# A linear-attention and bilinear feed-forward kernel: the same steps and loads in another written-out order

## The chip, the core and the metric

The kernel runs on one core of a Trainium2 chip. The core has a matrix engine (TensorE, PE in the profile; its weight loads are shown apart as PEld), a vector engine (VectorE, DVE), a scalar engine (ScalarE, ACT), a general engine (GpSimd, POOL) and a queue engine that only issues transfers (SyncE, SP). Each has its own list of instructions and works through it in the order written; semaphores make one wait for another. Sixteen DMA engines move data between the chip's memory and the on-chip buffer. Matmul results go to PSUM, eight banks of 512 float32 columns by 128 rows. The metric is the device time in microseconds (us) of one execution.

## The reference

Two parts follow each other: a gated linear attention, step by step over the sequence, and a feed-forward block without an activation function, in which two products are multiplied element by element.

```python
B, H, S, D = 4, 8, 768, 48          # q, k, v, alpha: [B, H, S, D]
for t in range(S):
    state = alpha[:, :, t, :, None] * state + einsum('bhd,bhe->bhde', k[:, :, t], v[:, :, t])
    y[:, :, t] = einsum('bhd,bhde->bhe', q[:, :, t], state)
x = y.transpose(0, 2, 1, 3).reshape(B * S, H * D)     # [3072, 384]
out = ((x @ w_a) * (x @ w_b)) @ w_out                 # w_a, w_b: [384, 1536], w_out: [1536, 384]
```

## The kernel before

**Staging.** The sequence of 768 steps is cut into three stretches of 256, and the four batches into two pairs. That gives six chunks: chunk c holds stretch c // 2 for the batch pair c % 2 (line 503). Inside a chunk `u` is the batch of the pair (0 or 1), and `g` the half of the stretch. Steps are held in pairs (`r`), so that 128 rows hold 256 steps. Within a chunk the recurrence becomes matmuls: decays are summed in logarithms, queries and keys are scaled by their exponentials, scores between steps are masked and multiplied with the values, and a state carries what came earlier from one half or stretch to the next. The chunk's output is written transposed (`xT`, 384 features by 512 steps), and the feed-forward part runs on it: 12 slices `f` of 128 hidden columns.

**The order.** Nothing is planned when the program is built. The string `PROGRAM` (line 17) lists all operations in the order in which they are issued, with the number of the chunk ahead of the colon; lines 1033 to 1038 walk through it and call one small function per operation. The last letter of many operations names the engine: V vector, S scalar, P GpSimd, Y SyncE. A number at the end of a matmul operation is its PSUM bank; an operation that takes two banks names the first. Since each engine keeps the order of the list, the list settles what stands behind what on every engine and on the transfer queues of POOL and SP. An outside planner wrote the list with its own costs and rules; it is not part of the kernel.

The operations that the next sections name are these (function and line behind them):

- `ld`, `W`, `Wo`: loads of alpha, k, q, v (510), of columns of w_a and w_b (493), of rows of w_out (497). `cz`, `cs`, `cm`: constants. `fill n`: n dummy matmuls (538).
- `ln`, `ra`: logarithm and inverse of alpha on ACT (518, 606). `l2`, `l2s`: sums of two steps' logarithms (524, 575). `H`, `L`, `R`: the sums split into parts that the matmul takes without loss (560, 569, 584). `B`, `A2`, `AQ`: running sums by matmul (551, 601, 591). `E`: their exponentials on ACT (620).
- `lv`: k or q scaled by alpha or its inverse (613). `mk`, `mq`: k and q scaled by the exponentials (635). `dk`, `de`, or `dr`, `dl`: the decay over a half, by matmul and ACT (658, 684) or by two transfers (646, 653).
- `C`, `Ce`: a turn (transpose) by TensorE and its copy out of PSUM (696, 706). `T`, `Tr`: the turn by a transfer on SP and a copy (712, 715).
- `v`, `vs`: values cast and swapped between halves (732, 741).
- `K`, `K2`: the state's matmuls (750, 762), `k`: the state's update on vector (778).
- `D`: scores (798). `M`: scores masked by vector out of PSUM (812); or `Mc`, a copy by ACT (816), and `Mm`, the mask by vector (820).
- `SA`, `SB`: the part of the output from the state, `Y`: the part from the scores (837, 852). `X`: the copy to `xT` (864), for one half (`u`) of its columns.
- `a f w`, `b f w`: slice f of x @ w_a and x @ w_b, three matmuls each (885). w is `*` for all 512 columns of `xT`, or 0 or 1 for 256 of them. `as`: the copy of `a` by ACT (891). `pr`: the product of that copy with `b` by vector, into `prod` (897).
- `o m h`: half of the 12 matmuls of output rows m (905), `ot`: their copy out (930), `st`: the store (943). `oc`, `otc`, `stc`: the same for half the columns of the last rows.

Buffers are few. A PSUM bank is taken again as soon as the operation that empties it is done, so `pr`, `as`, `k`, `M`, `Ce`, `X`, `ot` and `E` let later matmuls go. `as` has three buffers (line 894), `ot` four (931), `prod` and `xT` two, the loaded tiles two for each tensor (403).

The lines that carry most of PE's time are one loop each:

```python
for kk in range(KT):          # 3; line 889
    nc.tensor.matmul(p, lhsT=(wa_t, wb_t)[w][:, kk, f * 128:(f + 1) * 128], rhs=ch.xT[:, kk, us, :], start=(kk == 0), stop=(kk == KT - 1))
for f in range(half * NFF // 2, (half + 1) * NFF // 2):     # 6; line 911
    nc.tensor.matmul(op, lhsT=ch.prod[:, f, at:at + C], rhs=wo_t[:, f, :], start=(f == 0), stop=(f == NFF - 1))
```

Of the kernel before, what the change touches and what calls it, by code (L numbers as in the profile page):

```python
# [17 lines left out]
0: cm 0; c1; cz 0 b P; ci; ld a 0b Y; c1a; ld a 0a Y; ln 0b; cu; cz 1 b P; fill 7 0; cu2 V; cz 0 q V; cus; ld k 0b Y; ld k 0a Y; B 0b 2; ln 0a  # L18
# [4 lines left out]
0: v 0 S; vs 0 1 S; B 1a 6; E 1a i; M 0 0  # L23
1: ld a 1 P
0: E 1a b; W a 768 1536; c2 P; vs 0 0 V; B 1b 4; W b 768 1536; dk 1 6; E 1b i; M 0 1
1: ld q 0 P
0: Y 0
1: ld k 0 P
0: mk 1a V; SA 0; E 1b b; mq 1a V; mk 1b V; C 1 0 7; K 1 1 2; mq 1b V; Ce 1 0 V; C 1 1 3; v 1 S; Ce 1 1 V; de 1; K 1 0 4; k 1 0 V; k 1 1 V; D 1 0 6; X 0 S
0: a 2 0 0; a 4 0 1; Mc 1 0; vs 1 1 V; as 4 0; vs 1 0 V; a 5 0 3; D 1 1 4; Mc 1 1; SB 1 6; Mm 1 1 V; a 1 0 1; Mm 1 0 V; b 4 0 2; as 1 0; pr 4 0; a 3 0 4; as 3 0  # L30
0: b 0 0 1; K 0 1 5; SA 1; Y 1; a 0 0 2; as 2 0; b 2 0 0; k 0 1 V; X 1 S; b 3 0 4; pr 3 0
1: ln 0; l2 0 P
0: b 1 0 5; pr 1 0; a 4 1 6; pr 2 0
1: ln 1
0: b 5 0 7
1: ld v 0 P; H 0 V
0: as 0 0; pr 0 0; as 5 0; pr 5 0
1: l2 1 P
0: a 2 1 4
1: ld q 1 P  # L40
0: Wo 0 6; a 1 1 5; a 0 1 0; as 0 1
1: ra 0; lv 0 q P
0: b 0 1 2; pr 0 1; a 10 * 3; a 7 * 0; as 4 1; b 4 1 1
1: L 0 V
0: pr 4 1; b 2 1 2; as 7 *
1: ld k 1 P
0: as 2 1; as 10 *
1: ra 1
0: pr 2 1
1: H 1 V  # L50
0: b 1 1 6; b 5 1 7; b 7 * 4
1: L 1 V
0: pr 7 *
1: A2 0 0; E 0 i; E 0 b; mq 0 V
0: b 10 * 1; pr 10 *
1: lv 0 k P
0: Wo 6 12; as 1 1; pr 1 1; a 8 * 2; a 5 1 3; as 5 1; pr 5 1; b 3 1 0; b 9 * 4; a 6 * 3
1: A2 1 5; E 1 b; E 1 i
0: a 9 * 1
2: ld a * P  # L60
1: mk 0 V
0: a 3 1 6; as 3 1; pr 3 1; a 11 * 7
1: dk * 5
0: as 8 *; as 9 *; pr 9 *
1: ld v 1 P; C 0 1 2; lv 1 q P
2: ld q * P
0: as 6 *
1: lv 1 k P; Ce 0 1 S; C 0 0 6; Ce 0 0 V
2: ld k * P
1: de *  # L70
0: b 8 * 0; pr 8 *
3: ld v * P
0: cz 1 v P
1: v 0 S
0: as 11 *; c3 P
1: vs 0 1 S
0: b 11 * 1; pr 11 *; b 6 * 2; pr 6 *
1: K2 0 0 0 3; k 0 0 V; D 0 0 4; Mc 0 0; Mm 0 0 V
0: o 2 0 6
1: mq 1 V  # L80
0: o 3 0 7
1: SB 0 0; vs 0 0 S
3: ld a * P
1: mk 1 V; D 0 1 4; M 0 1
0: o 1 0 2; o 1 1 -; ot 1 S
1: k 0 1 V
0: o 3 1 -
1: C 1 1 2; C 1 0 4
0: ot 3 V
1: Ce 1 1 V  # L90
0: st 3 Y
2: ln *; l2s 0 P
0: o 2 1 -
1: K2 1 1 5 7; Ce 1 0 V; D 1 1 2; Y 0; v 1 S; SA 0
0: o 0 0 4; o 0 1 -
1: vs 1 0 S
2: l2 0 V
1: Mc 1 1
2: l2s 1 V; R 0
1: X 0 S; a 4 0 0; vs 1 1 S; k 1 0 V  # L100
0: cs 1 0 P; ot 0 S; st 0 Y
2: R 1; ra 1
1: a 2 0 1
2: lv 1 q P
1: as 4 0; k 1 1 V; as 2 0; D 1 0 2; M 1 0
2: AQ 4; E 0 i
1: b 4 0 7; a 6 0 0
2: E 1 b
1: b 6 0 1; a 1 0 2; pr 4 0
0: ot 2 V  # L110
1: b 1 0 3; as 6 0; pr 6 0; as 1 0; pr 1 0
2: ra 0
1: b 2 0 0; pr 2 0
# [120 lines left out]
3: SA 0
4: lv 0 k V
5: ld k * Y
4: E 1 b
3: Y 0
4: ld v * P; E 0 b
3: SA 1  # L240
1: st 0 Y
2: o 1 0 3; o 1 1 -
4: mk 1 V; mq 0 V
3: X 0 S
4: mq 1 V
3: X 1 S; b 11 * 7
4: E 0 i; mk 0 V
5: ln *
2: ot 0 V
3: a 11 * 6; as 11 *; pr 11 *; a 0 * 0; as 0 *; b 0 * 2; pr 0 *  # L250
4: v 1 S
3: b 8 * 1
2: ot 1 V
3: a 8 * 0; as 8 *
5: l2s 1 P
3: a 6 * 2; as 6 *
5: l2s 0 V; ra 0
3: a 2 * 3; a 9 * 0; as 9 *; b 6 * 2
4: T 0; dr
5: l2 0 P  # L260
3: a 3 * 4; pr 8 *
4: vs 1 0 S
5: R 0; R 1; ra 1
4: Tr 0 V; v 0 S
3: pr 6 *
5: lv 1 q P
3: b 9 * 5; pr 9 *; a 1 * 0; b 2 * 1; as 2 *
4: T 1
3: pr 2 *
5: AQ 6; E 1 i  # L270
4: dl; D 0 0 2; M 0 0
3: as 1 *
5: E 0 i
3: as 3 *; b 1 * 5; pr 1 *; a 5 * 1; as 5 *
5: lv 0 k P
3: a 4 * 0
# [24 lines left out]
5: mq 0 V
4: Mm 1 0 V
3: a 7 * 3; as 7 *; a 10 * 7; as 10 *
2: st 3 Y
4: vs 1 1 S
3: o 3 0 2; o 2 0 3; pr 10 *
4: Y 0; SA 0; X 0 S; Mm 1 1 V
5: mk 0 V
2: st 0 Y
4: SA 1; Y 1; X 1 S  # L310
5: T 0; mk 1 V; T 1; v 0 S
3: b 7 * 6; o 0 0 7
# [756 lines left out]
```

## Time and profile before

| | us |
|---|---|
| median of 3 runs | 192.12 |
| lowest and highest of them | 192.12, 193.25 |
| the profiled execution | 191.33 |
| its span, first to last instruction | 189.5 |
| PE busy in the span | 183.1 |
| DVE busy | 135.3 |
| ACT busy | 117.2 |
| POOL busy | 57.7 |

One execution was recorded. Its page gives busy times by engine, and views of the trace group instructions by line and shape, list who waited for whom, follow back the chain of work that ended last, and print an engine's instructions in order of time. "L889" is line 889 of the kernel. In a row of the timeline the first two numbers are the start and the duration in us, and a bracket names idle time of the engine ahead of the instruction and what ended it. A row of the groups ends with the busy time, the mean duration in ns, and the idle time ahead. The start of a row on an engine that is never idle is a better measure of what an instruction costs there than its duration, since neighbours overlap a little. The granted clock was 1.000 in the whole span.

### The profile page before, as it was taken

The page shows a single profiled execution, that of the slowest core. Times are in us where ns is not written, and L with a number is a line of the kernel's source. Part 1 is how long each engine was busy: PE and PEld are TensorE (multiplying, and loading weights), DVE is VectorE, ACT ScalarE, POOL GpSimd, SP SyncE. Part 2 cuts the span into 40 slices and gives each one's busy share as a digit, 9 for nine tenths or more (in the row PEclk, how much of TensorE's full clock was granted, in tenths as well). Part 3 has the DMA queues.
Part 4 walks back from the last instruction along what each step waited for, and adds up shares of the span by engine and source line. Part 5 has one row for each costly group of instructions (what it writes and reads, how often), then busy time and mean ns, then how long its engine had stood idle before and what let it go on. Part 6 is the DMA issues. An engine that isn't in the chain of part 4 may idle for free.

```text
span 189.5 us, 6112 instructions
## 1 busy us (share of the span) xinstructions
PE 183.1 (97%) x2597; PEld 114.6 (60%) x2613; DVE 135.3 (71%) x246; ACT 117.2 (62%) x220; POOL 57.7 (30%) x81
## 2 busy tenths in 40 slices
PE   7999899999999999999999999999999999999993
PEld 3888676656688776644457544646446454545563
DVE  2477778679898999797899898995287753144511
ACT  4497586896978996667475979747625524320610
POOL 8999177985154000203930226002000000000000
PEclk9999999999999999999999999999999999999999
DMA  5999999999999799988999396926902100002123
GB/s 130 265 223 199 263 241 248 237 258 268 236 220 194 102 190 263 266 231 154 208 267 206 93 159 134 127 85 71 175 27 83 45 3 0 0 5 83 42 83 125
DMA packets 64475, 29.41 MB, mean 155 GB/s; under 512 B 55760, under 2 KB 62816, under 8 KB 64448
## 3 DMA queue, kind: packets, MB, share of 16 engines
q1 hardware_dynamic: 46080, 16.34, 40.9%
q0 software_dynamic: 18224, 12.58, 38.8%
q8 instruction: 20, 0.33, 0.7%
q10 hardware_dynamic: 144, 0.10, 0.2%
q14 instruction: 7, 0.06, 0.1%
HBM read 25.98 MB, written 4.74 MB: 162 GB/s over the span
## 4 chain that ended last, share of the span: by engine, by line
PE 88%; DMA 4%; DVE 3%; issue 2%; POOL 2%; ACT 1%; POOLq 0%; ACTq 0%
PE psum L889 47%; PE psum L911 24%; PE psum L834 6%; DMA a_t<-in_alpha_dram 4%; PE psum L805 2%; PE psum L704 2%; PE psum L599 1%; DVE prod L903 1%; PE psum L922 1%; PE psum L773 1%; PE psum L760 1%; PE psum L666 1%; PE psum L557 1%; PE psum L558 1%; DVE vx L928 1%
## 5 line engine op out<-in xcount | busy, mean ns | idle before, releaser
L889 PE MATMUL psum<-xT,wb_t 128*128 128x512 bf16 (+1 forms) x261 | 54.7, 335 | 1.1 <-DVE vx L928 0.4
L889 PE MATMUL psum<-xT,wa_t 128*128 128x512 bf16 (+1 forms) x264 | 54.7, 336 | 0.4 <-issue 0.2
L911 PE MATMUL psum<-wo_t,prod 128*128 128x384 bf16 x276 | 49.2, 326 | 0.1
L889 PEld LDWEIGHTS <-wa_t 128*128 128x128 bf16 x270 | 25.8, 98 | 20.1 <-issue 0.2
L889 PEld LDWEIGHTS <-wb_t 128*128 128x128 bf16 x270 | 25.6, 98 | 19.6 <-DMA wb_t<-in_moe_w_b_dram 0.7
L911 PEld LDWEIGHTS <-prod 128*128 128x128 bf16 x276 | 26.2, 98 | 17.9
L926 ACT ACTIVATE ot<-psum 128x384 f32<-128x384 f32 (+1 forms) x12 | 5.7, 478 | 17.9 <-PE psum L911 15.3
L618 POOL TENSOR_TENSOR q_t<-q_t,ra 128x384 f32<-128x384 f32 x7 | 7.0, 1007 | 28.0 <-ACT ra L611 26.9
L926 ACT ACTIVATE vx<-v_t 32x384 bf16<-32x384 bf16 x28 | 14.6, 521 | 0.5
L579 POOL TENSOR_TENSOR l<-la 64x384 f32<-64x384 f32 x6 | 6.0, 994 | 26.0 <-PE psum L889 11.3
L818 ACT ACTIVATE m<-psum 128x768 bf16<-128x768 f32 x14 | 11.0, 810 | 3.2 <-PE psum L805 3.1
L928 DVE COPY ot<-psum 128x384 f32<-128x384 f32 (+1 forms) x13 | 7.0, 536 | 7.5 <-PE psum L911 7.0
L814 DVE TENSOR_TENSOR m<-psum,mask 128x768 bf16<-128x768 f32 x10 | 9.5, 952 | 1.8 <-PE psum L805 1.2
L522 ACT ACTIVATE la<-a_t 128x1536 f32<-128x1536 f32 (+2 forms) x9 | 9.4, 1053 | 2.0 <-DMA a_t<-in_alpha_dram 2.0
L870 ACT ACTIVATE xT<-psum 128x768 bf16<-128x768 f32 x10 | 7.9, 811 | 4.1 <-PE psum L834 3.9
L644 DVE TENSOR_TENSOR QKp<-q_t,beta 128x768 bf16<-128x768 f32 x10 | 9.4, 952 | 0.6 <-POOL q_t L618 0.6
L644 DVE TENSOR_TENSOR QKp<-k_t,invb 128x768 bf16<-128x768 f32 x10 | 9.6, 968 | 0.4 <-ACT invb L633 0.2
L834 PE MATMUL psum<-m,vx 64*64 64x64 bf16 (+1 forms) x576 | 8.7, 205 | 0.0
L515 POOL DMA_DIRECT2D v_t<-in_v_dram x8 | 8.7, 1087 | 0.0
L834 PEld LDWEIGHTS <-vx 64*64 64x64 bf16 x576 | 7.6, 108 | 0.6 <-issue 0.5
L737 ACT ACTIVATE vx<-v_t 128x768 bf16<-128x768 bf16 x9 | 7.5, 838 | 0.3 <-DMA v_t<-in_v_dram 0.2
L822 DVE TENSOR_TENSOR m<-m,mask 128x768 bf16<-128x768 bf16 x14 | 7.4, 551 | 0.4 <-ACT m L818 0.3
(278 smaller groups left out, 300.5 us busy)
## 6 DMA issues: line engine op xcount, KB each, us to landing
out_dram<-ot SPq DMA_DIRECT2D x23, 192.0 KB, 2.0
q_t<-in_q_dram SPq DMA_DIRECT2D x3, 768.0 KB, 6.0
k_t<-in_k_dram SPq DMA_DIRECT2D x3, 768.0 KB, 12.1
a_t<-in_alpha_dram POOLq DMA_DIRECT2D x2, 768.0 KB, 11.9
v_t<-in_v_dram POOLq DMA_DIRECT2D x4, 384.0 KB, 8.2
a_t<-in_alpha_dram SPq DMA_DIRECT2D x2, 768.0 KB, 6.7
a_t<-in_alpha_dram POOLq DMA_DIRECT2D x3, 384.0 KB, 7.8
k_t<-in_k_dram POOLq DMA_DIRECT2D x3, 384.0 KB, 7.4
```

The lines of the kernel that those rows point to most:

```text
L515: eng.dma_start(out=t[:, us, hs].rearrange("p b h r d -> p (b h) (r d)"), in_=src[ch.b0 + us.start:ch.b0 + us.stop, hs, ch.s * 2 * C:(ch.s ...
L522: nc.scalar.activation(out=ch.la[:, us, hs].rearrange("p b h r d -> p (b h r d)"), in_=ch.a[:, us, hs].rearrange("p b h r d -> p (b h r d) ...
L644: eng.tensor_mul(QKp[ch.c % 2][:, u, j, :, hs, :D], src[:, u, hs].rearrange("p h r d -> p r h d"), f)
L737: nc.scalar.activation(out=o_, in_=i_, func=AF.Copy)
L814: nc.vector.tensor_mul(m, x, maskn())
L818: nc.scalar.activation(out=m, in_=x, func=AF.Copy)
L834: nc.tensor.matmul(o, lhsT=lhsT, rhs=rhs, start=(g, c) not in begun, stop=False, skip_group_check=True)
L870: nc.scalar.activation(out=o_, in_=i_, func=AF.Copy)
L889: nc.tensor.matmul(p, lhsT=(wa_t, wb_t)[w][:, kk, f * 128:(f + 1) * 128], rhs=ch.xT[:, kk, us, :], start=(kk == 0), stop=(kk == KT - 1))
L911: nc.tensor.matmul(op, lhsT=ch.prod[:, f, at:at + C], rhs=wo_t[:, f, :], start=(f == 0), stop=(f == NFF - 1))
L926: nc.scalar.activation(out=o_, in_=i_, func=AF.Copy)
L928: eng.tensor_copy(o_, i_)
```

## The change

Only `PROGRAM` changes; every function stays. The new list has the same 872 operations, apart from two things: for 58 of them another engine is named, and many use another PSUM bank. The list was written by the same planner with two other inputs: it counted longer instruction fetches, and it weighed a placement by the mean of three cases of waits. The order differs from the second line on. The parts of the diff that are spoken of below, whole lines:

```diff
-0: ld q 0b Y; B 0a 0; E 0b i; mk 0b V; ld v 0 P; ld q 0a Y; ld a 1 P; cs 0 m P; ld k 1 P; ld q 1 P; cm 1; E 0b b; dk 0 2; E 0a i; mq 0b V; C 0 1 3; W b 0 256; cz 0 v P
-0: ld v 1 P; mk 0a V; E 0a b; fill 2 0; W a 256 768; cz 1 q P; W a 0 256; mq 0a V; C 0 0 1; Ce 0 1 S; Ce 0 0 V; K 0 0 0; de 0; W b 256 768; D 0 1 2; D 0 0 4; cs 1 m P; ln 1
-0: k 0 0 V; SB 0 0
+0: ln 0a; B 0a 0; ld v 0 P; ld q 0a Y; E 0b i; mk 0b V; ld a 1 P; dk 0 4; cs 0 m P; ld k 1 P; ld q 1 P; cm 1; W b 0 256; E 0b b; mq 0b V; cz 0 v P; E 0a i; mk 0a V
+0: fill 2 5; E 0a b; mq 0a V; ld v 1 P; C 0 1 0; W a 256 768; cz 1 q P; W a 0 256; C 0 0 1; Ce 0 0 V; de 0; W b 256 768; cs 1 m P; K 0 0 2; Ce 0 1 S; D 0 1 4; D 0 0 0; k 0 0 V
+0: SB 0 2; ln 1; B 1a 6
...
-0: a 2 0 0; a 4 0 1; Mc 1 0; vs 1 1 V; as 4 0; vs 1 0 V; a 5 0 3; D 1 1 4; Mc 1 1; SB 1 6; Mm 1 1 V; a 1 0 1; Mm 1 0 V; b 4 0 2; as 1 0; pr 4 0; a 3 0 4; as 3 0
-0: b 0 0 1; K 0 1 5; SA 1; Y 1; a 0 0 2; as 2 0; b 2 0 0; k 0 1 V; X 1 S; b 3 0 4; pr 3 0
+0: mq 1b V; C 1 1 4; K 1 1 5; X 0 V; D 1 0 2; Mc 1 0; a 3 0 0
+0: a 1 0 6; a 4 0 7; Ce 1 1 V; b 1 0 4; as 3 0; vs 1 1 V; as 4 0; D 1 1 2; Mc 1 1; k 1 0 V; k 1 1 V; Mm 1 0 V; SB 1 0; a 5 0 7; a 2 0 5; as 2 0; Mm 1 1 V; b 0 0 2
+0: b 3 0 3; K 0 1 5; pr 3 0; as 1 0
...
-1: K2 1 1 5 7; Ce 1 0 V; D 1 1 2; Y 0; v 1 S; SA 0
-0: o 2 1 -
-1: X 0 S; a 4 0 0; vs 1 1 S; k 1 0 V
+1: D 1 1 0; Y 0; X 0 S; K2 1 1 3 7; k 1 0 V
+1: k 1 1 V
+1: Mc 1 1; Mm 1 1 V
+0: o 2 1 -; ot 2 S
+1: a 10 0 3; a 2 0 4; a 4 0 5; as 2 0
...
-4: Y 0; SA 0; X 0 S; Mm 1 1 V
+3: SA 0; Mm 0 0 V; Y 0
+4: X 0 V
...
-5: as 9 *; o 0 0 0; o 3 0 1; pr 9 *; o 0 1 -; o 2 0 6
+5: b 7 * 0; as 7 *; o 3 0 2; o 0 0 7; pr 10 *; pr 7 *; o 0 1 -; ot 0 S; st 0 Y; o 3 1 -; o 2 1 -; ot 2 S; ot 3 V; st 3 Y; oc 1 1 1 -; otc 1 1 V; st 2 Y; stc 1 1 S
```

Chunk 1's `lv 0 k` and `lv 1 k` go from P to V. On chunk 3, `vs 0 1` goes from S to V. On chunk 4, `X 0`, `v 1` and `vs 1 0` go from S to V, and `l2s 0`, `lv 1 k` and `lv 1 q` from P to V; `Tr 1` and `vs 0 1` go from V to S. On chunk 5, `l2s 1`, `l2 0` and `lv 1 q` go from P to V, and `lv 0 q` from V to P.

More of the change, by code (lines that the diff above doesn't have):

```diff
@@ L52 @@
+1: dk * 7
+0: as 2 1
+2: ld a * P
 1: L 1 V
[L53 to L65, printed above, removed]
-2: ld q * P
-0: as 6 *
-1: lv 1 k P; Ce 0 1 S; C 0 0 6; Ce 0 0 V
+0: b 2 1 4; pr 3 1
+1: ld v 1 P; H 0 V; L 0 V
+0: a 10 * 2; as 10 *
@@ new lines @@
+2: D 1 1 6; M 1 1
+1: b 7 1 3; pr 7 1
+2: Tr 0 S
+1: b 1 1 0; b 0 1 1
+3: l2s 0 V
+1: a 1 1 2; as 1 1; pr 1 1
+2: D 1 0 4
+1: pr 0 1
+2: D 0 0 6; Mc 0 0
+1: o 0 0 3
+2: vs 0 0 V
+1: o 0 1 -
+2: Mm 0 0 V; Mc 1 0; SB 0 0; SB 1 4; D 0 1 6
+1: o 3 0 2
+4: ld a * Y
+2: Mc 0 1
+3: R 0
+1: o 3 1 -
+3: R 1
+1: ot 0 V
+3: AQ 6
+2: Mm 1 0 V; Mm 0 1 V; vs 1 0 S; SA 0; Y 1; vs 0 1 V
+1: ot 3 S
+3: E 0 b
+2: Y 0
+3: E 1 b; ra 0; ld q * Y; lv 0 q P; vs 1 0 V
+2: SA 1; X 1 V
+3: ld k * Y; lv 1 k V; lv 0 k V
+4: ld k * Y
@@ new lines @@
+1: o 1 0 2; o 1 1 -; st 3 Y
+2: X 0 S; a 4 * 3; b 4 * 0
+3: E 0 i; ra 1; lv 1 q V; mq 1 V; E 1 i
+2: b 0 * 1; a 9 * 4
+3: mk 1 V
+2: a 5 * 5
+4: ln *; l2s 0 V; ra 0
+2: a 0 * 6; a 3 * 7
+3: mq 0 V
+2: as 4 *; a 6 * 3; as 9 *
+3: mk 0 V
+2: pr 4 *
+3: dr
+2: b 9 * 4
+4: ld q * Y
+2: b 5 * 0; as 5 *; pr 9 *; as 0 *; pr 0 *
+3: v 0 S; K2 * * 6 5
+2: b 3 * 4; pr 5 *; as 3 *; pr 3 *
+3: vs 0 0 S
+0: st 2 Y
+3: dl; k * 0 V
+1: ot 1 S
+3: T 0
+0: cs 0 0 P
+1: st 2 Y
+2: b 6 * 1; a 11 * 0; as 6 *; pr 6 *; as 11 *
@@ L236 @@
+4: R 0; R 1
 5: ld k * Y
-4: E 1 b
[L238 to L264, printed above, removed]
@@ new lines @@
+4: v 1 V
+3: a 6 * 0
+4: Tr 0 V
+3: as 6 *; as 5 *
+4: vs 1 0 V
+3: b 6 * 1; pr 6 *
+4: K * 0 3; D 0 1 4; M 0 1
+5: AQ 6; E 0 i; lv 0 q P
+3: b 5 * 2; pr 5 *; b 11 * 0
+5: lv 0 k P; E 1 b; E 1 i
+1: st 1 Y
+4: dl; k * 0 V
+2: o 3 0 1
+5: ra 1
+3: pr 11 *
+2: o 3 1 -; ot 3 V
+4: SB 0 2; Tr 1 S; D 0 0 4; M 0 0
+2: st 1 Y
+5: E 0 b
+4: D 1 1 6; Mc 1 1
+5: lv 1 q V
+3: a 0 * 0; as 0 *
+2: st 3 Y
+3: b 0 * 1
+5: ld v * P
+3: pr 0 *
+4: Mm 1 1 V
+5: mk 0 V
+4: SB 1 4; D 1 0 6; Mc 1 0; vs 0 1 S
+3: b 7 * 0; a 10 * 1
```

458 lines of the change are left out of this document (194 added, 264 removed).

## The prediction

> **What bounds the kernel now.** I read the page's first part, then who waited on TensorE, then the chain that ended last. The reader is to see one engine full, and how little of its span is waiting.
>
> ```profile
> span 189.5 us, 6112 instructions
> ...
> PE 183.1 (97%) x2597; PEld 114.6 (60%) x2613; DVE 135.3 (71%) x246; ACT 117.2 (62%) x220; POOL 57.7 (30%) x81
> ```
>
> ```profile
> PE psum L540 <- DVE og L440: 1.2, 1, 1.2
> PE psum L889 <- issue: 0.5, 3, 0.2
> PE psum L889 <- DVE vx L928: 0.4, 1, 0.4
> PE psum L760 <- issue: 0.2, 1, 0.2
> ```
>
> ```profile
> 50.42 0.66 PE psum L889 x6
> ...
> 154.07 8.37 PE psum L889 x38
> ...
> 178.66 5.85 PE psum L911 x36
> ...
> 186.57 0.33 ACT ot L926
> ```
>
> The four waits of PE are all it has: 2.3 us, of which 1.2 lie ahead of its first instruction. Busy could hide waiting, as matmul ends are modelled, so I look at spacing: 38 matmuls of 512 columns took 8.37 us, 220 ns each, and 36 of 384 columns 5.85 us, 162 ns each. That is 2.3 to 2.4 columns per ns in both, so nothing hides between them. PE runs without a hole from the head to 186.5, and what follows (copy of the last half row and its store, 189.5 - 186.5 = 3.0 us) is there in both programs. So the order can win only the 1.1 us of waits behind PE's first instruction. The profiled execution took 191.33 us, 1.8 more than its span. The median of the runs is 192.12, 0.8 more; I make the sum on 191.33 and add 0.8.
>
> **What the change leaves alone.** Counting the two lists, every PE operation of before is in after, 323 of them, as often and with the same tiles, so PE's 183.1 us of work stay. The changes between 64-row and 128-row matmuls are as many. The loads and their halves are the same, the DMAs on POOL's queue stand in the same sequence, and on SP's only stores (st), dr and T change places. The first `a` or `b` product of chunks 1, 2, 3 and 5 comes after the same amount of PE work; chunk 4's comes about 1 us of PE work (one half of an output, six of the 162 ns) sooner. So the skeleton stands, and the sum is over hand-offs: whether what PE asks for next is there.
>
> **Gain at the first products.** One wait of PE is a load's.
>
> ```profile
> 20.57 0.50 PE L889 MATMUL psum<-xT,wb_t 128*128 128x256 bf16 x3 [0.43 <-DVE vx L928]
> ```
> ```profile
> 13.24 0.77 POOL L495 DMA_DIRECT2D wb_t<-in_moe_w_b_dram  x1
> ```
> ```profile
> wb_t<-in_moe_w_b_dram POOLq DMA_DIRECT2D x1, 384.0 KB, 7.3
> ```
>
> The row names vector, but the product `b 4 0` is the first to read columns 256 to 768 of w_b, and these land at 13.24 + 7.3 = 20.5. After puts `b 1 0` (columns 0 to 256) first and `b 3 0` behind seven other half products, about a microsecond later. I take the whole 0.43 as won. The 0.2 before L760 has no releaser: bounds 0 and -0.2, I take -0.1.
>
> **The head.** After moves both dummy matmuls (fill) ahead of the first turn `C 0 1`, and `Ce 0 1` behind `de 0` on ACT. `ln 1` follows there, and `B 1a` waits for it.
>
> ```profile
> 8.50 0.62 PE L704 MATMUL psum<-ident,QKp 128*128 128x128 bf16 x8
> 8.96 0.38 PE L540 MATMUL psum<-wz 128*128 128x512 bf16 x1
> ...
> 9.39 0.61 PE L704 MATMUL psum<-ident,QKp 128*128 128x128 bf16 x8
> ```
> ```profile
> 9.16 1.02 ACT L926 ACTIVATE kqT<-psum 128x1024 bf16<-128x1024 bf16 x1 [0.52 <-PE psum L704]
> 10.08 0.34 ACT L687 ACTIVATE bl<-psum 48x8 f32<-48x8 f32 x2
> 10.73 0.84 ACT L522 ACTIVATE la<-a_t 128x768 f32<-128x768 f32 x1 [0.31 <-DMA a_t<-in_alpha_dram]
> ```
>
> Both fills fit between 8.96 and 9.39. The turn then ends near 8.50 + 0.43 + 0.62 = 9.55, and its copy at 9.55 + 0.92 = 10.5 (0.92 from 9.16 to 10.08), ahead of the alpha load that lets `ln 1` go at 10.73. That load hides the move. I take **0**, with an upper end of 0.2 in case the scores, which wait for the copy, push `B 1a`.
>
> **Loss at chunk 1's first product.** ACT must copy xT's first half (`X 0`) before `a 10 0`. Before, PE began chunk 1 at 50.42.
>
> ```profile
> L515 POOL DMA_DIRECT2D a_t<-in_alpha_dram x1: 1161/1161/1161, 34.2 to 34.2; - x1
> ...
> DMA to landing us min/median/max: 10.3/10.3/10.3
> ```
> ```profile
> 44.31 0.49 ACT L926 ACTIVATE ot<-psum 128x384 f32<-128x384 f32 x1 [1.75 <-PE psum L911]
> 44.70 1.48 ACT L522 ACTIVATE la<-a_t 128x1536 f32<-128x1536 f32 x1
> 46.08 0.83 ACT L737 ACTIVATE vx<-v_t 128x768 bf16<-128x768 bf16 x1
> 46.94 1.06 ACT L926 ACTIVATE vx<-v_t 32x384 bf16<-32x384 bf16 x2
> 48.02 0.81 ACT L818 ACTIVATE m<-psum 128x768 bf16<-128x768 f32 x1
> 48.73 0.80 ACT L870 ACTIVATE xT<-psum 128x768 bf16<-128x768 f32 x1
> 49.55 1.05 ACT L926 ACTIVATE vx<-v_t 32x384 bf16<-32x384 bf16 x2
> ```
>
> Starts show what each costs in a row of them: ot 0.39, ln 1.38, v 0.86, vs 1.08, Mc 0.71, X 0.82. After asks ACT, from chunk 2's alpha on (34.2 + 10.3 = 44.5), for `ln *`, `ot 1`, `Ce 1 1`, `v 1`, `vs 1 0`, `ot 0`, `X 0`: 1.38 + 0.39 + 0.92 + 0.86 + 1.08 + 0.39 + 0.82 = 5.84, ready at 50.3. PE, which keeps the 0.43, would come at 50.42 - 0.43 = 50.0. Behind `X 0` queue `Mc 1 1`, `ot 2` and the first `as`. Before, X was done at 49.53, 0.9 early: the cover is used up. Bounds 0 and 0.9 (if alpha lands later, each us is one of PE); I take **0.3**.
>
> **Operations that change engine.** 58 operations are given to another engine: 30 come to vector (19 from ACT, 11 from POOL), 25 leave it (20 to ACT, 5 to POOL). Counted by the rows below and their likes, vector's work grows by about 3.5 us, POOL's falls by about 7, ACT's grows by 1. By chunk vector gets +1.3 (1), -1.7 (2), +1.8 (3), +2.5 (4) and under 0.5 elsewhere.
>
> ```profile
> L618 POOL TENSOR_TENSOR k_t<-k_t,a_t 128x384 f32<-128x384 f32 x5 | 5.0, 1007 | 0.5 <-DMA k_t<-in_k_dram 0.5
> ...
> L618 DVE TENSOR_TENSOR k_t<-k_t,a_t 128x384 f32<-128x384 f32 x5 | 2.8, 555 | 0.1
> ...
> L872 DVE CAST xT<-psum 128x768 bf16<-128x768 f32 x2 | 1.9, 958 | 3.0 <-PE psum L834 3.0
> ```
> ```profile
> L928 DVE COPY vx<-v_t 32x384 bf16<-32x384 bf16 x16 | 4.2, 263 | 0.4
> ```
> ```profile
> L644 DVE TENSOR_TENSOR QKp<-q_t,beta 128x768 bf16<-128x768 f32 x10 | 9.4, 952 | 0.6 <-POOL q_t L618 0.6
> ```
>
> Chunk 1's `lv 0 k` and `lv 1 k` go from POOL to vector, so a late load of k now holds all of vector's queue, where it held only POOL (0.5 us in that row). `mk`, both `mq` and the products `pr` stand behind; the banks that `pr` empties are what PE asks for. Before, the wait was 0.5 at most and vector reaches `lv 1 k` later than POOL did, so 0 to 0.5; I take 0.
>
> Where vector is full the additions count:
>
> ```profile
> 80.00:104.00 24.00, 23.71 (x358) 12.53 (x361) 21.81 (x35) 14.92 (x26) 7.75 (x9) 1.00 1.12 214
> 104.00:130.00 26.00, 25.68 (x399) 14.06 (x391) 23.70 (x38) 19.47 (x34) 5.10 (x5) 1.00 0.65 113
> 130.00:154.00 24.00, 23.76 (x341) 12.97 (x344) 13.86 (x24) 12.14 (x22) 0.99 (x2) 1.00 0.42 78
> ```
>
> (columns: stretch, length, busy us of PE, PEld, DVE, ACT, POOL). From 80 to 130 vector is busy for 45.5 of 50. After adds here chunk 3's `vs 0 1` (2 x 0.263), chunk 4's `X 0` (0.958), `lv 1 k`, `lv 1 q` (0.555 each), `l2s 0`, `vs 1 0` (0.53), `v 1` and chunk 5's `lv 1 q`, `l2s 1`, `l2 0`; with 0.55 for each l2s and l2 and 0.3 for v, which are estimates after lv and vs, 5.7 in all. It takes out `Tr 1` and `vs 0 1` of chunk 4 and `lv 0 q` of chunk 5 (about 1.6, by the same rows and 0.5 for Tr), and puts `lv 1 k`, `mq 1`, `mk 1` of chunk 5 (0.555 + 2 x 0.952 = 2.5) behind 130, where ten of 24 us are free. Net +1.6: 47.1 of 50, and 4.5 us of idle shrink to 2.9.
>
> Three hand-offs have least room, found by adding up, between two points that PE sets, what vector is asked for.
>
> ```profile
> L589 DVE TENSOR_TENSOR ll<-lh 128x768 f32<-128x768 f32 x4 | 3.8, 954 | 0.1
> ```
> ```profile
> L790 DVE TENSOR_TENSOR tmp<-psum,Sm 128x192 f32<-128x192 f32 x4 | 1.4, 353 | 0.6 <-PE psum L760 0.6
> L791 DVE TENSOR_TENSOR S<-tmp,bl 128x192 bf16<-128x192 f32 x4 | 1.4, 358 | 0.1
> ```
>
> From chunk 1's `K2 1 1` to its `SB 1`, whose bank `k 1 1` must empty, PE has one `o` half, three half products and a set of scores: 0.98 + 3 x 0.33 + 0.2 = 2.2 (two half products took 0.66 at 50.42). Vector has `k 1 0`, `R 1`, `k 1 1`: 0.71 + 0.95 + 0.71 = 2.4, some 0.1 less for each by starts, as in ACT's rows: even. In the same way `k 0 1` comes about 0.3 ahead of the turn `C 1 0`, and chunk 3's `Mm 0 0`, last of ten operations from `pr 7` on, about 0.1 ahead of its `Y 0`. Each may cost 0 to 0.5; I take 0.1 each, **0.3**.
>
> **The end.** After's last product, `b 7 *`, is followed by the halves `o 3 0` and `o 0 0` (1.95 us of PE) before `o 0 1` needs its `pr 7`, with one more `pr` ahead of that in vector's queue.
>
> ```profile
> 178.74 0.73 DVE L903 TENSOR_TENSOR prod<-as__3418,psum 128x512 bf16<-128x512 bf16 x1 [0.29 <-ACT as__3418 L895]
> ```
>
> Two of these are 1.5, covered by 0.4. Behind stand the same quarter outputs, copies and stores as before. I take 0.
>
> **Sum.** -0.43 - 0.1 + 0 + 0.3 + 0 + 0.3 = +0.07 on 191.33 makes 191.4; with the 0.8 to the median, **192.2 us**. Ends: everything won (0.43, 0.2 and the 0.5 of the other waits of PE) and nothing lost, 190.2 and so 191.0 as a median; everything lost (0.2 + 0.9 + 0.5 + 1.5 - 0.43 = 2.7), 194.0 and so 194.8.
>
> **Rivals.** *Faster*: PE's 1.1 us go and every hand-off holds: 191.0. For it: most hand-offs come out even or early. Against: even this is 0.6%, and a gain over 1% (1.9 us; a per cent is about what a measurement of this kernel can tell from no change) needs PE work to shrink, which it cannot.
>
> *Slower: vector becomes the bound from 80 to 130.* It decides where vector cannot fill the 1.6 us that its idle time loses, because its waits there are for PE and for each other's results. If none can be filled, PE waits 1.6 more at the chain `R 0`, `R 1`, `Mm 1 1`, `Mm 0 0` before `AQ`, `Y 1`, `Y 0` of chunks 3 and 4: 192.2 + 1.6 = 193.8, and with ACT's upper end (0.6 more) and the head's (0.2) 194.6. For it: 91% and 91% busy. Against: 10 us are free behind 130, and `AQ` of chunk 5, which vector feeds, comes 2.1 us of PE work later than before. Beside the rows stands a rule of the Trainium skill (Perfetto Trace Analysis, Identifying the Most-Contended Engine): matmul busy is no good measure of closeness to the limit, weight-load busy is, and the engine with most occupancy is the one to relieve. By it PE stands at 60% and vector at 71%, and if all of vector's 3.5 us passed to the time it would be 195.7. The trace does not agree: the spacing above has PE full.
>
> *The change does nothing it says*: the order of loads is as it was and PE is full either way; that is my forecast with all terms at zero, 192.1.
>
> **Chances.** Forecast within 1%: 0.70, with the faster rival's 191.0 mostly in it; faster by over 1%: 0.05; slower by over 1%, the vector rival with a late load: 0.25. The range goes from 191.0 to 194.8 and leaves out some 2 in 10, most of it above.
>
> **What would show it.** PE busy at 183 and a span between 188.5 and 191; no wait of PE for wb_t near 20; `B 1a` near 11.6; `X 0` of chunk 1 ending near 50.3 with PE right behind; DVE busy about 139, over 92% from 80 to 130; POOL about 51. Wrong it would be made by one PE wait over 1 us, most likely on a vector `Mm`, `k` or `pr`, or by a load that lands later than before.

## The result, and the profile after

| | before | after |
|---|---|---|
| median, us (16 executions each, side by side) | 192.11 | 194.61 |
| lowest to highest | 191.26 to 193.31 | 192.63 to 195.50 |
| profiled execution | 191.33 | 193.29 |
| its span | 189.5 | 191.5 |

The ratio after to before is 1.0099, 95% interval 1.0075 to 1.0124: about 1% slower. Ratios leave out executions more than 1.5% above the fastest of their kernel: none here, five of eleven in the first repetition below. The medians lie a little further apart (1.013), since after's executions lie in two groups: five from 192.63 to 193.58, eleven from 194.20 up.

The page of after, span and busy times:

```profile
span 191.5 us, 6131 instructions
...
PE 184.3 (96%) x2613; PEld 114.4 (60%) x2613; DVE 138.9 (73%) x253; ACT 117.8 (62%) x221; POOL 50.6 (26%) x73
```

PE's work has not grown: the span less PE's waits and the 3.0 us behind PE's end is 184.2 us in before and 184.3 here. (Busy time is 1.2 higher; before's trace lacks 16 of the 2613 matmul records, which may be all of it.) Who waited on TensorE, in after (us in total, times, longest):

```profile
PE psum L518 <- DVE og L418: 1.2, 1, 1.2
PE psum L535 <- ACT la L500: 0.7, 1, 0.7
PE psum L812 <- issue: 0.7, 1, 0.7
PE psum L867 <- DVE prod L881: 0.5, 1, 0.5
PE psum L783 <- DVE kp L906: 0.5, 1, 0.5
PE psum L783 <- ACT kqT L904: 0.3, 1, 0.3
PE psum L738 <- issue: 0.3, 1, 0.3
```

(Line numbers are 22 lower than in before: L867 is L889 of before, L783 is L805, L812 is L834, L738 is L760.) Behind the first instruction PE waits 3.0 us, where it waited 1.1 in before: 1.9 more, and the span is 2.0 longer. The wait for w_b at 20.57 is not in the list; new are the head's waits (L783 on kqT, L535 on la, until 10.33 and 11.85), L867 on vector (until 87.08), L783 on the copy `Tr` (kp, until 98.16) and a stop in `Y` (L812, until 105.17) for which no releaser shows. The expectations below call the last three the waits at 86.2, 97.3 and 104.3.

The stretches of after (length, busy us of PE, PEld, DVE, ACT, POOL):

```profile
80.00:104.00 24.00, 23.03 (x265) 11.47 (x267) 21.98 (x37) 16.77 (x28) 3.29 (x4) 1.00 1.15 222
104.00:130.00 26.00, 25.34 (x443) 13.86 (x439) 23.09 (x39) 18.24 (x34) 3.14 (x3) 1.00 0.71 119
130.00:154.00 24.00, 24.00 (x282) 12.72 (x273) 16.62 (x28) 11.28 (x20) 1.25 (x2) 1.00 0.43 79
```

PE is full behind 130 and has three holes between 80 and 106. So I look at what feeds it there. The queue of SP in before and then in after:

```profile
68.82 7.51 SPq L515 DMA_DIRECT2D k_t<-in_k_dram  x2
...
84.98 0.88 SPq L944 DMA_DIRECT2D out_dram<-ot  x1
85.97 5.25 SPq L713 DMA_TRANSPOSE kqT<-QKp  x2
91.28 0.83 SPq L515 DMA_DIRECT2D a_t<-in_alpha_dram  x1
```
```profile
70.25 7.35 SPq L493 DMA_DIRECT2D k_t<-in_k_dram  x2
...
86.45 3.07 SPq L691 DMA_TRANSPOSE kqT<-QKp  x1
89.58 0.57 SPq L922 DMA_DIRECT2D out_dram<-ot  x1
90.20 2.93 SPq L691 DMA_TRANSPOSE kqT<-QKp  x1
93.17 0.69 SPq L493 DMA_DIRECT2D a_t<-in_alpha_dram  x1
```

Chunk 3's keys are asked for 1.4 us later. Its two turns by transfer (`T 0`, `T 1`) follow each other in before; in after a store stands between them, and the second is issued at 90.20, where in before it went at 88.78. Vector shows what that does, first in before, then in after:

```profile
79.55 0.56 DVE L618 TENSOR_TENSOR k_t<-k_t,a_t 128x384 f32<-128x384 f32 x1
...
95.44 1.40 DVE L928 COPY kp<-kqT 128x1024 bf16<-128x1024 bf16 x2
```
```profile
80.63 1.03 DVE L596 TENSOR_TENSOR k_t<-k_t,a_t 128x384 f32<-128x384 f32 x2 [0.92 <-DMA k_t<-in_k_dram]
...
97.67 0.43 DVE L906 COPY kp<-kqT 128x1024 bf16<-128x1024 bf16 x1 [0.79 <-DMA kqT<-QKp]
```

The keys hold vector for 0.9 us, and the second `Tr` waits for its transfer until 97.67. In before the second turn had landed at 93.60, 2.2 us before its copy began (95.77), and both copies had been made by 96.84. So the turn lands 4.1 us later in after, and only 1.4 of that is its later issue: it takes 7.45 us from the start of its issue where it took 4.82. The chain that ended last names both transfers, where in before it ran 88% through PE:

```profile
70.25 10.28 DMA k_t<-in_k_dram
...
90.20 7.45 DMA kqT<-QKp
...
97.67 0.44 DVE kp L906
```

### The profile page after: what moved, and what is told of

Read it like the earlier page. It is cut to its first block, busy times and chain, and to the rows that moved or that the text cites. A ratio compares the mean times of both kernels' runs of the same rounds, so it can differ in the third digit from the quotient of the medians.

```text
span 191.5 us, 6131 instructions
## 1 busy us (share of the span) xinstructions
PE 184.3 (96%) x2613; PEld 114.4 (60%) x2613; DVE 138.9 (73%) x253; ACT 117.8 (62%) x221; POOL 50.6 (26%) x73
## 4 chain that ended last, share of the span: by engine, by line
PE 76%; DMA 13%; DVE 3%; ACT 2%; issue 2%; POOL 1%; SPq 1%; POOLq 0%; DVEq 0%
PE psum L867 41%; PE psum L889 20%; DMA k_t<-in_k_dram 5%; PE psum L812 5%; DMA kqT<-QKp 4%; DMA a_t<-in_alpha_dram 4%; PE psum L783 2%; DVE QKp L622 1%; PE psum L682 1%; SPq L493 1%; PE psum L900 1%; PE psum L751 1%; PE psum L577 1%; PE psum L644 1%; PE psum L738 1%
## 5 line engine op out<-in xcount | busy, mean ns | idle before, releaser
L867 PE MATMUL psum<-xT,wb_t 128*128 128x512 bf16 (+1 forms) x270 | 55.6, 337 | 0.5 <-DVE prod L881 0.5
L867 PE MATMUL psum<-xT,wa_t 128*128 128x512 bf16 (+1 forms) x270 | 55.0, 337 | 0.0
L889 PE MATMUL psum<-wo_t,prod 128*128 128x384 bf16 x276 | 49.0, 326 | 0.0
L867 PEld LDWEIGHTS <-wa_t 128*128 128x128 bf16 x270 | 25.8, 98 | 20.1 <-issue 0.2
L867 PEld LDWEIGHTS <-wb_t 128*128 128x128 bf16 x270 | 25.6, 98 | 19.5 <-issue 1.4
L889 PEld LDWEIGHTS <-prod 128*128 128x128 bf16 x276 | 26.2, 98 | 18.3
L904 ACT ACTIVATE ot<-psum 128x384 f32<-128x384 f32 (+1 forms) x15 | 7.2, 479 | 13.6 <-PE psum L889 12.3
L906 DVE COPY ot<-psum 128x384 f32<-128x384 f32 (+1 forms) x10 | 5.3, 534 | 13.0 <-PE psum L889 12.0
L904 ACT ACTIVATE vx<-v_t 32x384 bf16<-32x384 bf16 x26 | 13.5, 521 | 0.5
L812 PE MATMUL psum<-m,vx 64*64 64x64 bf16 (+1 forms) x576 | 8.9, 205 | 0.7 <-issue 0.7
L812 PEld LDWEIGHTS <-vx 64*64 64x64 bf16 x576 | 7.8, 107 | 1.3 <-issue 1.1
L906 POOL COPY vx<-v_t 32x384 bf16<-32x384 bf16 x2 | 1.2, 624 | 26.8 <-ACT vx L715 26.8
L812 PE MATMUL psum<-kqT,Sm 64*64 64x128 bf16 x144 | 7.6, 219 | 0.0
L848 ACT ACTIVATE xT<-psum 128x768 bf16<-128x768 f32 x7 | 5.4, 808 | 2.2 <-PE psum L812 2.2
```

The lines of the kernel that those rows point to most:

```text
L812: nc.tensor.matmul(o, lhsT=lhsT, rhs=rhs, start=(g, c) not in begun, stop=False, skip_group_check=True)
L904: nc.scalar.activation(out=o_, in_=i_, func=AF.Copy)
L906: eng.tensor_copy(o_, i_)
```

## The experiments

My first theory (**late load**): SP reaches chunk 3's keys late, vector stands still, and everything up to the masks of chunk 3 is late. Rivals: the **turn** alone (the store between the two turns), **vector full** (the prediction's rival), the **head** (the alpha load), and, from the second row of runs on, **blocks of program** (TensorE's own instructions come late). A rival that was not set up, the load of v that POOL issues beside the second turn, is taken up behind the run that gives work back to POOL. Each row of runs was made beside the kernel before on one chip.

### The changed kernel once more

> The changed kernel once more, unaltered, beside the kernel before. Its executions lay in two groups, near 193 and near 194.7 us; the profiled one was of the lower. Late-load theory: chunk 3's keys landed at 80.5 us there, vector stood still for them 0.9 us, and PE lost 0.5 at 86.2, 0.4 at 97.3 and 0.85 at 104.3 behind that; the upper group is the same place with a later landing. So the median again some 2.5 us over before, in two groups, and where the profiled execution is of the upper group, the additional 1.5 us stand between 66 and 106. Head theory: they stand ahead of 20 us. Vector-full theory: the same waits in every execution, no groups from this cause.

Measured: median 195.0 (192.49 to 196.38) against 192.64, ratio 1.0082 (1.0039 to 1.0126). The profiled execution took 193.77. The wait until 87.08 is gone in it, kp costs 0.3, and a stop stands in `Y` of chunk 2 that the first profile didn't have:

```profile
77.30 0.40 PE L812 MATMUL psum<-m,vx 64*64 64x128 bf16 x20
78.80 0.89 PE L812 MATMUL psum<-m,vx 64*64 64x64 bf16 x64 [1.09 <-issue]
```

So the losses move between executions. This spoke against a single late load and gave the next question: what is a stop of 1.1 us that no semaphore ends?

### Keys ahead of alpha

```diff
-4: ld a * Y
...
-3: ld k * Y; lv 1 k V; lv 0 k V
+3: ld k * Y
+4: ld a * Y
+3: lv 1 k V; lv 0 k V
```

> Chunk 4's alpha load moved on the queue of SP from ahead of chunk 3's load of q and k to behind that of k: 768 KB, 3 us at 260 GB/s, so chunk 3's keys should land near 77.6 instead of 80.5. Late-load theory: vector no longer stands still before its scaling of the keys (0.9 us), PE's wait at 86.2 goes, the turn at 97 and the one at 104 shrink; 1 to 1.8 us under the unaltered changed kernel in the lower group, and the upper group goes: median 192.2 to 193. Vector-full theory: vector then waits as long elsewhere, under 0.4 us gained. Head theory: nothing gained.

Measured: median 194.23 (192.81 to 194.76), ratio 1.0097 (1.0059 to 1.0135). Vector no longer waited for the keys:

```profile
80.13 1.01 DVE L597 TENSOR_TENSOR k_t<-k_t,a_t 128x384 f32<-128x384 f32 x2
...
97.94 0.43 DVE L907 COPY kp<-kqT 128x1024 bf16<-128x1024 bf16 x1 [1.21 <-DMA kqT<-QKp]
```

and the first turn was issued 0.5 us sooner (85.94); yet the second `Tr` came at 97.94. The late load is real, but it is not what costs: my first theory falls.

### The store behind both turns

```diff
-1: st 2 Y
...
 3: T 1
+1: st 2 Y
```

> Chunk 1's store of output rows 2 moved on the queue of SP from between chunk 3's two turns by transfer to behind the second, as in the kernel before. The second turn is then issued at 89.6 instead of 90.2 and lands 0.6 earlier, at 97.05 instead of 97.65. Turn theory (this store makes the wait at 97.3 and pushes the masks at 104.3): 0.5 to 1.0 us under the unaltered changed kernel. Late-load theory: 0.3 to 0.6, since the keys are late as before and the groups stay. Head theory: nothing.

Measured: median 193.0 (191.69 to 193.96), ratio 1.0020 (0.9988 to 1.0053): 0.6% or 1.2 us under the unaltered kernel by the ratios, whose intervals overlap a little, and no longer to be told from before. (By the medians it is 2.0, the figure that later expectations use.) The queue of SP and vector's copies in it:

```profile
87.09 5.72 SPq L691 DMA_TRANSPOSE kqT<-QKp  x2
92.86 0.57 SPq L922 DMA_DIRECT2D out_dram<-ot  x1
```
```profile
97.12 0.75 DVE L906 COPY kp<-kqT 128x1024 bf16<-128x1024 bf16 x2
```

PE has no wait for kp in this profile and no stop at 104; of the stops the one near 77.5 is left (0.93). With this edit alone most of the loss is gone. Why is less clear: the second turn, issued at 89.61, still took 7.71 us to land.

### Two scalings back to POOL

```diff
-4: AQ 6; E 1 i; lv 1 k V; E 0 i
+4: AQ 6; E 1 i; lv 1 k P; E 0 i
...
-4: lv 1 q V
+4: lv 1 q P
```

> Chunk 4's scaling of the keys and queries of the second batch (lv 1 k, lv 1 q) given back from vector to POOL, as in the kernel before: vector has 2 x 0.55 us less between 102 and 105, ahead of the mask Mm 0 0 of chunk 3. Vector-full theory: PE's stop of 0.85 us at 104.3 goes, and 0.8 us of the time with it, in both groups. Late-load theory: the same stop goes here (0.6 to 0.85), since it is the vector queue through which a late load reaches PE, but the waits at 86.2 and 97.3 and the two groups stay.

Measured: median 193.83 (193.51 to 194.03), ratio 1.0083 (1.0056 to 1.0109), no gain by the ratio. The stop at 104.5 stayed (0.5), so it was no want of vector, and a new wait of 0.5 for `prod` ended at 96.47. Vector in this kernel, and the same two operations in after:

```profile
93.55 1.06 DVE L769 TENSOR_TENSOR S<-tmp,bl 128x384 bf16<-128x384 f32 x1
94.62 1.04 DVE L906 COPY vx<-v_t 32x384 bf16<-32x384 bf16 x2
```
```profile
93.33 0.56 DVE L769 TENSOR_TENSOR S<-tmp,bl 128x384 bf16<-128x384 f32 x1
93.91 0.52 DVE L906 COPY vx<-v_t 32x384 bf16<-32x384 bf16 x2
```

Both take twice as long, while POOL scales q (93.20 to 94.20) and issues a load (94.14 to 95.34). Work taken off vector came back as slower vector work (138.2 us busy against 138.9, with two operations of 0.55 fewer).

The same run shows something that none of the theories asked about. PE's wait for kp is gone from its profile. On POOL the load of chunk 4's v stands behind the two scalings, in before and here. In before it was issued at 95.24; the change takes the scalings (and two copies) off POOL, and the load goes beside the second turn (90.20); here it goes late again. The issue in after and then here:

```profile
90.33 1.20 POOL L493 DMA_DIRECT2D v_t<-in_v_dram  x1
```
```profile
94.14 1.20 POOL L493 DMA_DIRECT2D v_t<-in_v_dram  x1
```

From 95 to 97 in after, the transfers' view has 0.32 MB on the queue of POOL's loads (q0) and 0.03 on that of SP's transfers (q1), where the turn is still under way; here it has none on the first and 0.59 on the second, and the turn has landed at 94.74, 5.13 us after its issue at 89.61. No run moves this load alone, but the table of all profiles below has the same split in every one.

### Blocks of program

The stops without a releaser always stood at the same matmul: the same place in `Y` of chunk 2, of chunk 3, and in `K` (L738). The page's transfers have a queue that carries instructions:

```profile
q8 instruction: 20, 0.33, 0.7%
```

20 packets with 0.33 MB; over PE's 2613 matmuls and 2613 weight loads that is 63 bytes an instruction, and some 260 instructions a packet of 16 KB. The places of the stops agree: counted in weight loads, they stand at the 356th (`K` at 22.6), the 1253rd (`Y` of chunk 2) and the 1638th (`Y` of chunk 3), that is 7 and 3 times 128 and one apart, and 128 loads with their 128 matmuls are 256 instructions. The 0.2 ahead of L760 in before stands at the 356th too, and every stop over 0.16 us without a releaser, between 15 us and the end and in all profiles of the new order, lies a multiple of 128 from it, give or take two. For the block used from 77.5 on, the view of the transfers in a tenth of a microsecond: the first row is of after (from 74.3 to 74.4; no stop), the second of the kernel run once more (76.1 to 76.2; PE goes on at 78.80):

```profile
q8 instruction: 1, 0.02, 78.7%
```
```profile
q8 instruction: 1, 0.02, 77.4%
```

The later packet is there by 77.4, and PE goes on 1.4 us after that. At 104.5 of after the packet runs from 102.5 to 103.7, and PE goes on at 105.17: 1.5. To test it I moved the borders between blocks:

```diff
-0: cm 0; c1; cz 0 b P; ci; ld a 0b Y; c1a; ld a 0a Y; ln 0b; cu; cz 1 b P; fill 7 0; cu2 V; cz 0 q V; cus; ld k 0b Y; ld k 0a Y; B 0b 2; ld q 0b Y
+0: cm 0; c1; cz 0 b P; ci; ld a 0b Y; c1a; ld a 0a Y; ln 0b; cu; cz 1 b P; fill 1 0; warm 46 0; cu2 V; cz 0 q V; cus; ld k 0b Y; ld k 0a Y; B 0b 2; ld q 0b Y
```

> The changed kernel with six of the seven dummy matmuls ahead of the first work replaced by 46 short ones (128 columns): 80 more instructions for TensorE at a place where it waits for data anyway, so every later border between two 256-instruction blocks of its program comes 40 matmuls sooner. Instruction theory: TensorE stops at 77.5 and 104.5, without any semaphore, because the next 16 KB of its program have not come: they are asked for when a border is passed, start 1 to 4.6 us later behind the loads, take 1.2 us and are usable some 1.4 us after that. With the shift the pairs of borders with the shortest way between them lie 2.0 us apart (from 76.6) and 3.6 (from 102.6), 4.4 from 15.5 and 4.4 from 48.5, instead of 5.6 at the least; 5.5 to 7 are needed, so new stops of 2 to 4 us stand near 78.6 and 106, 1 to 2 near 20 and 53: 6 to 10 us slower. Data theory (the stops are waits for masks or values that the trace doesn't name): the stops stay at the same matmuls, within 1 us of the unaltered changed kernel.

Measured: one execution, 193.67. Its stops:

```profile
78.58 1.22 PE L812 MATMUL psum<-m,vx 64*64 64x128 bf16 x96
```
```profile
PE psum L783 <- issue: 0.6, 1, 0.6
...
PE psum L812 <- issue: 0.2, 1, 0.2
```

All 96 matmuls of `Y` of chunk 2 run through (as they did in after itself). The stop of 0.6 now stands at 21.8 in scores (L783), where none was, and `Y` of chunk 3 stops 0.2 at another matmul. By the count the first is again at the 356th weight load, the second at the 1766th, 11 times 128 and two further. So the stops go with the borders, and the data theory falls. My size was wrong: no 6 to 10 us came, since the packets at close borders started much sooner after, or even ahead of, the border. What sets the time of the request stays open.

### Parts of the change alone, in the kernel before

```diff
-0: a 2 0 0; a 4 0 1; Mc 1 0; vs 1 1 V; as 4 0; vs 1 0 V; a 5 0 3; D 1 1 4; Mc 1 1; SB 1 6; Mm 1 1 V; a 1 0 1; Mm 1 0 V; b 4 0 2; as 1 0; pr 4 0; a 3 0 4; as 3 0
+0: a 2 0 0; a 1 0 1; Mc 1 0; vs 1 1 V; as 1 0; vs 1 0 V; a 5 0 3; D 1 1 4; Mc 1 1; SB 1 6; Mm 1 1 V; a 4 0 1; Mm 1 0 V; b 1 0 2; as 4 0; pr 1 0; a 3 0 4; as 3 0
...
-0: b 1 0 5; pr 1 0; a 4 1 6; pr 2 0
+0: b 4 0 5; pr 4 0; a 4 1 6; pr 2 0
```

> The kernel before, with slices 1 and 4 exchanged in the first half products of chunk 0, so that the first product with w_b asks for its columns 128 to 256 and not for 512 to 640: this part of the change alone. If TensorE's wait at 20.57 was for the late columns, it goes, and 0.4 us of 192.1 with it (0.2%): 191.7. If another wait takes its place (the next load, vector), 0.0 to 0.2.

Measured: median 191.94 against 192.17, ratio 0.9976 (0.9944 to 1.0008). The wait at 20.57 is gone from its profile; one of 0.3 for later columns of w_b ends at 29.14. The size fits (0.2% was foreseen), but it cannot be told from nothing.

```diff
-1: ot 1 V; st 2 Y
+1: ot 1 V
...
 3: T 0; Tr 0 V
+1: st 2 Y
```

> The kernel before, with chunk 1's store of output rows 2 moved on the queue of SP from ahead of chunk 3's two turns by transfer to between them: the order that the change has there, alone. Turn theory (a store between the two turns makes the second land late, in many executions by over 1 us): 0.5 to 2.0 us slower than before, in two groups of times. Queue-sum theory (the second turn of the changed kernel was late only as all of SP's queue and vector were late by then): within 0.3 us of before, since here the first turn even gains 0.9 us.

Measured: median 192.17 against 192.17, ratio 0.9995 (0.9964 to 1.0025). A store between the turns costs nothing here, where the second turn took 4.48 us. The place of the store by itself is no cause.

### The store behind, and SP's queue sooner

```diff
-2: mk 0 V
+2: mk 0 V; mq 0 V
 1: as 10 1; pr 10 1; b 6 1 4; as 6 1; pr 6 1
-2: mq 0 V; T 1
+2: T 1
```

(with the store moved as above)

> The changed kernel with the store moved behind the second turn of chunk 3 (the edit that gave 2 us) and, besides, chunk 2's scaling mq 0 moved on vector from behind two products to behind mk 0: the turn that it feeds goes to SP's queue some 0.6 us sooner, and all loads behind it (chunk 4's alpha, chunk 3's q and k). Late-load theory: chunk 3's keys land at 79.9 and not 80.5, the stop near 77.5 shrinks by up to 0.6, and the median comes to 192.4 to 192.8, under 193.0. If SP's lateness there is no cause: 193.0, as with the store alone.

Measured: median 192.77 against 192.17, ratio 1.0012 (0.9982 to 1.0043). The profiled execution (192.22) has neither the stop at 77.5 nor those at 97 and 104. Against the store alone (1.0020) it can't be told apart.

### The store ahead of both turns, both edits together, and one more look

> The changed kernel unaltered, beside the two edits below on the same chip. By the two rows of runs so far: median 194.6 to 195.0, two thirds of the executions over 194, 2.3 to 2.5 us over before.

Measured: median 193.75 against 191.97, ratio 1.0073 (1.0039 to 1.0107); 1.8 us over before on this chip, not 2.3.

```diff
+1: st 2 Y
 3: T 0
 0: cs 0 0 P
-1: st 2 Y
```

> The changed kernel with chunk 1's store of rows 2 moved from between chunk 3's two turns to ahead of the first (moving it behind both gave 2 us). Both turns are then issued back to back; the first starts at 86.8 instead of 86.45, the second at 89.9 instead of 90.2, only 0.3 us sooner. Between theory (it is the store's place between the turns that makes the second late): nearly the whole 2 us again, median 193.0 to 193.4. Issue-time theory (each us by which the second turn is issued later is one of TensorE's): 0.3 us gained at most, median 194.3 to 194.7.

Measured: median 193.83 (192.94 to 195.24), ratio 1.0093 (1.0061 to 1.0125): no gain over the unaltered kernel beside it. With the same store moved in the kernel before, this ends the between theory. That it helps to have the store's issue and its 192 KB behind the turns is argued and not shown: the second turn took 7.77 us here and 7.71 with the store behind. In the profile (193.01) the second copy still waits 0.35, to 97.64, which PE just doesn't notice.

> Two edits that gained alone, together: the store behind both turns (2.0 us under the unaltered kernel) and chunk 4's lv 1 k and lv 1 q given back to POOL (1.2 us). One-cause theory (both cut the same late chain, second turn, copy Tr, scores, masks Mm of chunk 3 on vector): no more than the store alone, 192.6 to 193.2. Two-cause theory (late turn, and vector too full for itself): the sum, 191.8 or less, and then no slower than before.

(The edits of the third and fourth runs together.) Measured: median 193.26, ratio 1.0076 (1.0052 to 1.0100): by the ratios no gain over the unaltered kernel beside it, and less than the store alone had. Its profile has no wait for kp (the second turn took 4.73 us), but again the 0.5 for `prod`, until 96.37, beside POOL. Neither theory foresaw that: giving work back to POOL costs there.

> The changed kernel unaltered, one more look at where TensorE stops. Whatever group it falls in, I expect the stops without a semaphore at 77.5 and 104.5 (0.4 to 1.3 us, the next block of program late) and waits of 0.4 to 1.2 at 97 for the copy Tr; should it be an execution over 194.3, the 1 to 1.5 us beyond the other profiles stand at 97 to 106 if the chain through the second turn makes the upper group, and near 77 if the blocks of program make it.

Measured: 195.35, one of the longer executions. Its waits and its chain:

```profile
PE psum L783 <- DVE kp L906: 2.0, 1, 2.0
...
PE psum L812 <- issue: 1.1, 2, 0.5
```
```profile
89.99 9.64 DMA kqT<-QKp
```

The second turn was issued as in the others (89.99) and landed 9.64 us later instead of 7.45. In this one execution the slowest part is the turn; that it makes all the longer ones is likely, not shown.

Put together, from the lists of waits (us of PE on kp, and without a releaser in `Y`, L812) and from the traces (from the start of the second turn's issue to its landing; when POOL asked for chunk 4's v):

| profiled execution | time | kp | L812 | second turn took | v asked for at |
|---|---|---|---|---|---|
| changed, four times | 193.29, 193.77, 193.95, 195.35 | 0.5, 0.3, 0.9, 2.0 | 0.7, 1.7, 0.7, 1.1 | 7.45, 8.10, 8.34, 9.64 | 90.33, 89.80, 89.37, 89.46 |
| keys ahead | 193.80 | 0.9 | 0.8 | 8.31 | 88.97 |
| store behind | 192.58 | 0 | 1.1 | 7.71 | 89.89 |
| store behind, `mq 0` sooner | 192.22 | 0 | 0 | 8.44 | 88.65 |
| store ahead | 193.01 | 0 | 0.6 | 7.77 | 89.72 |
| borders moved | 193.67 | 0 | 0.2 | 8.02 | 90.15 |
| scalings on POOL | 193.51 | 0 | 1.3 | 5.13 | 94.14 |
| scalings on POOL, store behind | 193.12 | 0 | 0.4 | 4.73 | 94.04 |
| before | 191.33 | 0 | 0 | 4.82 | 95.24 |
| before with one part, twice | 191.50, 191.73 | 0, 0 | 0, 0 | 4.82, 4.48 | 95.40, 95.69 |

For the four of the changed kernel, 192.2 and the sum of kp and L812 gives 193.4, 194.2, 193.8 and 195.3, within 0.5 of each time. The two are not the whole account: the same sum is 0.7 too high for the store behind, and the 192.22 itself holds 1.4 us of other waits (alpha, `prod`, w_out). The last two columns split cleanly: with v asked for within 0.7 us of the second turn's issue, the turn took 7.45 us or more; with v asked for at 94.04 or later, 5.13 or less. In four of the nine the slow turn cost PE nothing: with `mq 0` sooner it was issued earlier (88.44), and in the others, it seems, PE came later itself.

## Why the prediction was right and wrong

The time came to 194.61 where 192.2 was forecast: inside the range, at its upper end. The ratio, 1.0099, is on the edge between no change (0.70) and slower by over 1% (0.25). The mechanism of that loss was in no step, so that the range holds it is luck: its upper end was added up from the head, `X 0`, a late load at chunk 1 and three hand-offs, and the loss came elsewhere.

- **What bounds it, right.** PE works as long as before, nothing shrank, and behind 105.17 PE has no wait in the list; the end costs 3.0 us in both (191.5 - 188.5).
- **The skeleton, wrong.** This is the step that failed. I wrote that the transfers on POOL's queue stand in the same sequence, and that on SP's only stores, `dr` and `T` change places, and left it at that. The sequence on POOL held, the times did not: with 7 us less to do, POOL asked for chunk 4's v at 90.33 and not 95.24, beside the second turn. The turns by transfer were in none of the hand-offs I summed. In before the second had 2.2 us to spare; in after it was issued 1.4 us later and took 2.6 us longer, and PE paid 0.3 to 2.0 in four executions. The sentence on what would make it wrong did name a wait of over 1 us, but on vector's `Mm`, `k` or `pr`, or a load.
- **The gain at the first products, right in kind.** The wait at 20.57 went; alone the reordering measured 0.2 us at the median, not to be told from nothing, and two other executions of the changed order still wait 0.2 and 0.3 for w_b at 21, so 0.43 was the upper end.
- **The 0.2 ahead of L760, wrong.** It did not go (0.3 in after): it stands where a block of program begins. In the changed kernel the same thing costs 0.7 at 104.5 and up to 1.1 at 77.7, terms that the sum didn't have. This is a second loss that the prediction put at nothing.
- **The head, right in kind.** `B 1a` came at 11.85 and not 11.6, because alpha landed at 10.95 and not 10.73. No edit is needed to explain it: in the kernel before with the moved store `B 1a` also waited 0.6, and in the changed kernel's first repetition it came at 11.57. The scores do wait 0.3 for the later copy, until 10.33, as the prediction's upper end allowed.
- **Chunk 1's first product, right.** `X 0` ended at 50.39 (49.58 + 0.81) against 50.3 foreseen, and PE began right behind it (50.45); by the starts PE lost 0 to 0.3 in the profiles, 0.3 was taken.
- **Engines, right.** DVE 138.9 and POOL 50.6, against 139 and 51. But vector was busy for 45.1 of 50 us from 80 to 130 (21.98 + 23.09), not 47.1. The estimates of single operations were not re-measured.
- **Three hand-offs at 0.1, not seen.** None of them shows a wait. The stop at chunk 3's `Y` looked like the third (mask `Mm 0 0`) and is a block of program.
- **The rival with vector as the bound, no.** Taking two operations off vector gained nothing. The weight-load share that the Trainium skill names (Perfetto Trace Analysis, Identifying the Most-Contended Engine) misleads here taken alone: PE's weight loads are busy for 60% in after too, and PE sets the time. The section names it together with the share of the peak in FLOPs, which is not worked out here.

## What to carry to other kernels

When a written order changes, follow every transfer that feeds a product as you follow the engines, with its queue, what stands ahead of it, and the time it has to spare. An engine that is given less to do issues its loads sooner: ask which transfers they will meet. A transfer that arrives just in time has a tail that a single profile doesn't show, so look at several executions. A stop of TensorE with no releaser in a phase of many small matmuls is to be held against the instruction queue in the transfers' view, and its place counted in instructions, before it is put down to data. Before work is moved to POOL, look at what vector does beside it.

## What the runs showed of the hardware

**TensorE's program comes late.** Its blocks of 256 instructions are packets of the same 16 DMA engines as the data (20 of them, 0.7% of the engines' span), and where TensorE stops it goes on 1.3 to 1.7 us after the packet's end; in phases of small matmuls that costs 0.2 to 1.1 us a border, at none to three of the borders in an execution. When the packets are asked for is not shown. The Trainium skill (Runtime: NRT & Kernel Launch, Instruction fetch mechanics) has the 16 KiB blocks and the engine's own queue, which agrees with the 20 packets here; it calls the cost mostly hidden, which holds for most borders here and not for the 1.09 us at 78.80.

**POOL slows vector.** A product of two on-chip operands went from 0.56 to 1.06 us beside a POOL operation, and a pair of copies from 0.52 to 1.04 beside POOL's load issue. The Trainium skill (GPSIMD Engine Reference, Key points) says that POOL shares its interfaces to the buffer with vector, and that they contend for vector's operations in a two-port mode or with two inputs from it; for the product the trace agrees, with a doubling, and in which mode the copies ran it does not show.

**A turn by transfer is slow beside a load of POOL.** From the start of its issue to landing, the same second turn took 4.48 to 5.13 us in the five profiles where the load of v came later, and 7.45 to 9.64 us in the nine where it was asked for within 0.7 us of the turn. No run moved the load alone.
